# A causal convolution and two feed-forward layers on one core: earlier first transfers, zero matmuls at the start, one [high; low] stationary for the last 64 channels, the weight bound on two engines

## The chip, the cores and the metric

One core of one Trainium2 chip. The metric is the device time of one execution in microseconds. The kernel before takes 1337.52 us (median of 3 runs, 1336.18 to 1337.96); its profiled execution took 1334.66 us, of which the program's span is 1332.8 us.

## The reference

```python
w = softmax(weight, axis=-1)                     # 8 heads x 7 taps
x1 = causal_conv(x, w)                           # x: 2 x 4096 x 192, 24 channels per head
h = x1 @ w_in1                                   # 8192 x 192  @  192 x 2048
g = h * clip(h + 3, 0, 6) / 6
x2 = g @ w_out1                                  # 2048 x 192
h = x2 @ w_in2
P = a0 + a1*h + a2*h**2 + a3*h**3
Q = 1 + |b0|*|h| + |b1|*h**2
out = (P / (Q + 1e-6)) @ w_out2                  # 8192 x 192, float32
```

x is float32; the four weight matrices arrive as 64-bit floats.

## The kernel before

**Tiles.** The 8192 tokens are cut into chunks of 512 (the last one into two of 256), tokens in the free dimension and channels on the partitions. The 192 channels do not fit 128 partitions: "A" is channels 0 to 127, "B" the last 64. The 2048 hidden channels are 16 tiles f of 128. Every number is carried as a high part (rounded to the type fp32r) and a low part (the rest), and a product is high x high + low x high + high x low, so one hidden tile costs five matmuls of 128x512 in `product_in` (L481: Ah·ah, Al·ah, Ah·al and two for B) and five in `product_out` (L495 to L500).

**B before.** For layer 1 the moving tile x1b is [high; low] of the 64 channels, and the stationary tiles are Bh = [high; high] and Bl = [low; 0]. For layer 2 the moving tiles are x2m2 = [a copy of the high part; low] and x2m1, and the stationary ones Bh = [high; high] and Bl = [low; high]. `hi_w` therefore copies each piece of a weight tile twice into Bh (L369, L370) and, in layer 2, a third time into Bl (L372).

**Weights.** Each 64-bit weight is turned into a 32-bit float on the chip, per tile "in" (512 or 256 columns) or "out" (384): ACT takes the magnitude of the upper word into a box m (`mag_w`, L328), POOL bounds it between two limits (`clamp_w`, L337), DVE does three bit operations into PSUM bank 2 or 3 (`bits_w`, L349, L352, L356), ACT rounds to the high parts (`hi_w`, L363 to L372), DVE subtracts for the low parts (`lo_w`, L380). There are 16 "in" and 16 "out" tiles over both layers, and this decoding runs beside the first two chunks' layer 1.

**Start.** The filter: `weight` is loaded (tap), DVE computes the softmax into `line`, `line` is written to memory (line_d, L879) and read back as a band matrix (L268), both on ACT's queue. `conv` (L428) multiplies band with x (xn, loaded at L415, L418 on SP's queue), ACT evicts (`conv_ev`, L436), `flip` (L443) transposes, ACT and DVE make the high and low parts (L448; x1al L454, x1b L457). Chunks 0 and 1 go through this one after the other, through the same banks 0 and 1 (bank_93 and bank_94 in the lists of instructions below), before the first `product_in`.

**Steady state.** Layer 1 of one chunk and layer 2 of an earlier one are interleaved, tile by tile. A layer-1 tile costs two ACT, one DVE and one POOL instruction (L525, L530, L537, L543), a layer-2 tile about seven ACT, five DVE and two to three POOL instructions. At the end of a chunk `x2_op` (L554 to L562) takes the accumulators acc00 and acc01 to the tiles of layer 2.

**Order.** No engine's order is written out. `Issue.order` sorts all operations with tables of offsets (OFF, OFF0, OFFT, W1P, W2P, WPART, XW ...) and durations written in the code, and lets an engine take a ready operation out of turn within a look-ahead (AHEAD, LOOK). Changing any table changes the order on all engines. The DMA queues of SP and ACT are in order too: an issue that waits holds all issues behind it.

Of the kernel before, what the change touches and what calls it, by code (L numbers as in the profile page):

```python
# [46 lines left out]
X0 = -3.5576  # L47
XW = [-98.6812, -95.7871, -90.8177, -84.1979]
BIAS = dict(l1=1.5372, dec=1.797, conv=1.4061, out=-0.7086, x2=3.0264)
AHEAD = dict(P=4.733, A=25.052, V=17.217, G=15.336, S=999.0)  # L50
LOOK = dict(P=3, A=156, V=132, G=410, S=0)
OFF = dict(
    sq=-0.2391, q1=-0.0381, q2=0.2567, mm3=-0.423, mm1=0.8404, mm4=0.4459, tr=0.6018, mm2=0.8241, A=-0.3233,
    t1=0.075, u=0.9885, R=0.5331, RR=0.6369, hi2=1.4938, hi1=1.9951, S=-0.1322, lo2=1.926, lo1=2.8291,
    q=-3.2594, t2=0.1782, t3=0.4844, w=0.7884, p2=0.8597, G=0.9565, g=1.2626, cv=0.9616, x1ah=1.0094,
    x1al=1.7783, x1bh=1.0281, x1bl=1.2078, x2ah=1.7232, x2al=2.0125, x2mh=1.2801, x2mc=2.4281, x2ml=1.7914,
    oa=0.6663, oc=0.8609, os=1.4993, mm2l=1.1909, mm4l=0.5848,
# [875 lines left out]
```

## Time and profile before

| | us |
|---|---|
| device time, median of 3 | 1337.52 |
| profiled execution | 1334.66 |
| its span | 1332.8 |
| PE busy | 1268.9 (95%) |
| ACT busy | 1188.3 (89%) |
| DVE busy | 1172.6 (88%) |
| POOL busy | 1127.3 (85%) |
| first matmul of the convolution | at 15.50 |
| first `product_in` of layer 1 | at 28.68 |
| first `product_in` of layer 2 | at 126.49 |

A matmul's record is longer than the distance between two starts, so the busy time of PE in a stretch hides short gaps; where that matters, matmuls are counted and multiplied by the distance. The waits of an engine are put down to whoever came last by the records.

### The profile page before, as it was taken

What the parts mean: (1) busy time and instruction counts of PE and PEld (TensorE: products, weight loads), DVE (VectorE), ACT (ScalarE), POOL (GpSimd) and SP (SyncE); (2) the same over time, 40 slices, a digit from 0 to 9 for tenths busy, and PEclk for the clock granted to TensorE, in tenths of its full rate; (3) what the DMA queues carried; (4) which work ended last, traced back from release to release, by engine and by line L of the source; (5) the groups of instructions that cost most, each with busy time, mean ns of one, the idle gap of its engine ahead of it and who ended that gap; (6) DMA issues with size and microseconds to landing.
All of it is one profiled execution on the core that took longest, in us unless ns stands there. A gap on an engine that the chain in (4) does not pass through costs nothing.

```text
span 1332.8 us, 18555 instructions
## 1 busy us (share of the span) xinstructions
PE 1268.9 (95%) x6048; PEld 1042.9 (78%) x6048; DVE 1172.6 (88%) x1824; ACT 1188.3 (89%) x2174; POOL 1127.3 (85%) x932
## 2 busy tenths in 40 slices
PE   4988999999999999999999999999999999999977
PEld 3766887878878888788878888788788888887766
DVE  5888889899898988889999899988889888898897
ACT  4878999999999999999999999999999999998886
POOL 3977888888888889898888888888888888888875
PEclk8999999999999999999999999999999999999998
DMA  6341000000000000000000000000000000000000
GB/s 194 103 130 48 16 0 14 14 9 20 1 26 2 13 16 13 15 7 7 15 12 16 13 16 9 5 16 12 16 13 1 13 1 1 12 1 12 1 13 12
DMA packets 28984, 28.61 MB, mean 21 GB/s; under 512 B 2140, under 2 KB 25816, under 8 KB 28888
## 3 DMA queue, kind: packets, MB, share of 16 engines
q1 hardware_dynamic: 27672, 26.74, 6.6%
q8 instruction: 47, 0.77, 0.2%
q10 hardware_dynamic: 1216, 0.70, 0.2%
q14 instruction: 49, 0.40, 0.1%
HBM read 21.13 MB, written 6.30 MB: 21 GB/s over the span
## 4 chain that ended last, share of the span: by engine, by line
PE 73%; DVE 9%; ACT 9%; POOL 5%; issue 3%; DMA 0%; ACTq 0%; DVEq 0%; POOLq 0%
PE bank L481 35%; PE acc L495 7%; PE acc L498 7%; PE acc L500 7%; PE acc L499 7%; PE acc L496 7%; PE bank L428 2%; DVE S L645 1%; DVE bank L649 1%; POOL g2l L669 1%; POOL S L625 1%; DVE T L654 1%; ACT bank L640 1%; POOL g1l L543 1%; PE bank L443 1%
## 5 line engine op out<-in xcount | busy, mean ns | idle before, releaser
L625 POOL TENSOR_TENSOR S<-A,S 128x512 f32<-128x512 f32 x252 | 326.9, 1297 | 57.7 <-ACT S L611 45.2
L669 POOL TENSOR_TENSOR g2l<-T,g2h 128x512 fp32r<-128x512 f32 x252 | 328.7, 1305 | 44.2 <-ACT g2h L660 42.0
L543 POOL TENSOR_TENSOR g1l<-u,g1h 128x512 fp32r<-128x512 f32 x240 | 312.0, 1301 | 26.3 <-ACT g1h L537 21.2
L645 DVE SCALAR_TENSOR_TENSOR S<-S,bank 128x512 f32<-128x512 f32 x252 | 172.8, 686 | 85.5 <-ACT bank L640 83.0
L631 DVE SCALAR_TENSOR_TENSOR T<-T,coef,bank 128x512 f32<-128x512 f32 x252 | 188.5, 748 | 8.8
L619 DVE SCALAR_TENSOR_TENSOR T<-T,coef,bank 128x512 f32<-128x512 f32 x252 | 187.0, 742 | 8.6 <-ACT T L604 7.2
L649 DVE SCALAR_TENSOR_TENSOR bank<-T,coef,bank 128x512 f32<-128x512 f32 x252 | 188.7, 749 | 0.0
L654 DVE SCALAR_TENSOR_TENSOR T<-S,bank 128x512 f32<-128x512 f32 x252 | 173.1, 687 | 8.5
L530 DVE SCALAR_TENSOR_TENSOR u<-u,bank 128x512 f32<-128x512 f32 x240 | 162.7, 681 | 16.5 <-ACT u L525 15.3
L636 ACT ACTIVATE A<-S 128x512 f32<-128x512 f32 x252 | 159.7, 634 | 18.2 <-POOL S L625 17.2
L604 ACT ACTIVATE T<-bank,coef 128x512 f32<-128x512 f32 x252 | 173.6, 689 | 1.6 <-POOL g2l L669 1.3
L660 ACT ACTIVATE g2h<-T 128x512 fp32r<-128x512 f32 x252 | 160.2, 636 | 12.5 <-DVE T L654 10.6
L640 ACT ACTIVATE bank<-A 128x512 f32<-128x512 f32 x256 | 154.2, 603 | 14.7 <-DVE T L631 8.7
L525 ACT ACTIVATE u<-bank 128x512 f32<-128x512 f32 x240 | 143.7, 600 | 22.4 <-PE bank L481 15.1
L537 ACT ACTIVATE g1h<-u 128x512 fp32r<-128x512 f32 x240 | 150.9, 633 | 4.1 <-PE acc L500 2.3
L613 POOL TENSOR_SCALAR S<-A,coef 128x512 f32<-128x512 f32 x126 | 97.9, 777 | 43.1 <-ACT A L592 42.1
L481 PE MATMUL bank<-x2ah,Ah 128*128 128x512 f32 (+1 forms) x272 | 106.4, 391 | 16.9 <-DVE T L654 16.6
L495 PE MATMUL acc<-g2l,O 128*128 128x512 f32 (+1 forms) x280 | 112.6, 404 | 4.2 <-POOL g2l L669 2.3
L481 PE MATMUL bank<-x1ah,Ah 128*128 128x512 f32 (+1 forms) x272 | 106.2, 390 | 5.9 <-DVE u L530 2.6
L498 PE MATMUL acc<-g2h,O 128*128 128x512 f32 (+1 forms) x280 | 109.4, 391 | 0.1
L500 PE MATMUL acc<-g2h,O 128*128 128x512 f32 (+1 forms) x280 | 107.4, 384 | 0.2 <-DVE oac L677 0.2
L499 PE MATMUL acc<-g2h,O 128*128 128x512 f32 (+1 forms) x280 | 107.3, 383 | 0.0
(122 smaller groups left out, 3301.6 us busy)
## 6 DMA issues: line engine op xcount, KB each, us to landing
raw<-in_moe_w_out_dram SPq DMA_DIRECT2D x16, 384.0 KB, 3.4
out_dram<-osb SPq DMA_DIRECT2D x32, 192.0 KB, 2.0
xn<-in_x_dram SPq DMA_DIRECT2D x14, 384.0 KB, 3.4
raw<-in_moe_w_in_dram SPq DMA_DIRECT2D x16, 256.0 KB, 2.8
raw<-in_moe_w_in_dram SPq DMA_DIRECT2D x16, 128.0 KB, 3.1
xn<-in_x_dram SPq DMA_DIRECT2D x16, 96.0 KB, 3.2
xn<-in_x_dram SPq DMA_DIRECT2D x2, 288.0 KB, 5.6
band<-line_d ACTq DMA_DIRECT2D x1, 512.0 KB
```

What stands on the lines that cost most here:

```text
L481: nc.tensor.matmul(out=dst[:, cs], lhsT=w[nm][:, fs], rhs=m, start=(k == 0), stop=(k == 4))
L495: nc.tensor.matmul(out=a, lhsT=o[:, 0:128], rhs=g, start=False, stop=sp)
L498: nc.tensor.matmul(out=a, lhsT=o[:, 0:128], rhs=g, start=st, stop=False)
L499: nc.tensor.matmul(out=a, lhsT=o[:, 256:384], rhs=g, start=False, stop=False)
L500: nc.tensor.matmul(out=c, lhsT=o[:, 128:256], rhs=g, start=st, stop=False)
L543: nc.gpsimd.tensor_tensor(out=gl, in0=v1.pop((b, i)), in1=f32(g1[b, i][0]), op=ALU.subtract)
L619: stt(out=d["T"], in0=d["T"], scalar=coef[:, 2:3], in1=h2[b, i], op0=ALU.add, op1=ALU.mult)
L625: (nc.gpsimd if k else nc.vector).tensor_tensor(out=d["S"], in0=d["A"], in1=d["S"], op=ALU.add if k == 1 else ALU.mult)
L631: stt(out=d["T"], in0=d["T"], scalar=coef[:, 1:2], in1=h2[b, i], op0=ALU.add, op1=ALU.mult)
L649: stt(out=h2[b, i], in0=v2[b, i]["T"], scalar=coef[:, 0:1], in1=h2[b, i], op0=ALU.add, op1=ALU.mult)
L654: stt(out=d["T"], in0=d["S"], scalar=2.0, in1=h2.pop((b, i)), op0=ALU.subtract, op1=ALU.mult)
L669: e.tensor_tensor(out=gl, in0=v2.pop((b, i))["T"], in1=f32(gh), op=ALU.subtract)
```

## The change

The diff, cut to what acts; all tables of offsets have other numbers, of which four lines stand here.

```diff
-CONV2 = 1.7151
+CONV2 = 0.8376
-LOENG = [0, 0, 0, 0]
-CLAMP = [1, 1, 1, 1]
+WARM = 5
+LOENG = [0, 1, 0, 1]
+CLAMP = [0, 1, 0, 1]
...
-    xt = ctx.enter_context(tc.tile_pool(name="xt", bufs=2))
+    xt = ctx.enter_context(tc.tile_pool(name="xt", bufs=3))
...
+    idle = cst.tile([128, C], F32, name="idle")
+    def warm():
+        if not spare:
+            spare.append(pa.tile([128, C], F32, tag="acc11", name="warm"))
+        nc.tensor.matmul(out=spare[0], lhsT=idle[:, 0:128], rhs=idle, start=True, stop=True)
...
     def load_band():
-        nc.scalar.dma_start(
+        nc.sync.dma_start(
...
-            Bh=wts.tile([128, DFF], F32R, name=f"Bh{l}"), Bl=wts.tile([128, DFF], F32R, name=f"Bl{l}"),
+            B=wts.tile([128, DFF], F32R, name=f"B{l}"),
...
+    def bound_w(key):
+        r = raw[key]
+        e, m = (nc.gpsimd, r[2]) if CLAMP[side_of(key)] else (nc.vector, r[3])
+        e.tensor_scalar(out=m, in0=m, scalar1=LIM[0], scalar2=LIM[1], op0=ALU.max, op1=ALU.min)
+    def side_of(key):
+        return 2 * key[1] + (key[0] == "out")
...
-            act(out=w["Bh"][0:64, cs], in_=src, func=ACTF.Copy)
-            act(out=w["Bh"][64:128, cs], in_=src, func=ACTF.Copy)
-            if l == 1:
-                act(out=w["Bl"][64:128, cs], in_=src, func=ACTF.Copy)
+            act(out=w["B"][0:64, cs], in_=src, func=ACTF.Copy)
...
-            sub(w["Bl"][0:64, cs], m[hs, 256:512], w["Bh"][hs, cs])
+            sub(w["B"][64:128, cs], m[64 * part - 64:64 * part, 256:512], w["B"][0:64, cs])
...
+    low1 = [wts.tile([128, C], F32R, name=f"low1{k}") for k in range(3)]
+    low2 = [wts.tile([128, C], F32R, name=f"low2{k}") for k in range(3)]
+    def zero_low(k):
+        nc.gpsimd.memset(f32((low1 + low2)[k][64:128]), 0.0)
...
-        if l == 0:
-            seq = [("Ah", ah), ("Al", ah), ("Ah", al), ("Bh", bb), ("Bl", bb)]
-        else:
-            seq = [("Ah", ah), ("Al", ah), ("Ah", al), ("Bh", m2), ("Bl", m1)]
+        seq = [("Ah", ah), ("Al", ah), ("Ah", al), ("B", bh), ("B", bl)]
...
         elif nm == "x2mh":
-            act(out=t, in_=c, func=ACTF.Copy)
+            act(out=t[0:64], in_=c[0:64], func=ACTF.Copy)
+        elif nm == "x2mg":
+            act(out=t[64:128], in_=c[0:64], func=ACTF.Copy)
...
-            nc.vector.tensor_copy(out=t[0:64], in_=f32(x2[b, "x2m1"][0:64]))
+            nc.vector.tensor_tensor(out=t[0:64], in0=c[64:128], in1=f32(t[0:64]), op=ALU.add)
...
-        at(-100 + b if first else t - 8, "S", 1900, load_x, b, w=[("xn", b)], after=1700)
+        at(-100 + 45 * b if first else t - 8, "S", 1900, load_x, b, r=[("line_d", 0)] if b else [], w=[("xn", b)], after=1700)
...
-    at(-62, "A", 400, lambda: nc.scalar.dma_start(out=line_d, in_=line), r=[("line", 0)], w=[("line_d", 0)], after=1600)
-    at(-60, "A", 400, load_band, r=[("line_d", 0)], w=[("band", 0)], after=3600)
+    at(-62, "S", 400, lambda: nc.sync.dma_start(out=line_d, in_=line), r=[("line", 0)], w=[("line_d", 0)], after=1700)
+    at(-60, "S", 1800, load_band, r=[("line_d", 0)], w=[("band", 0)], after=1700)
...
+    for k in range(WARM):
+        at(-104 + 0.01 * k, "P", 900, warm, r=[("idle", 0)], w=[("acc11", "warm")])
```

B's stationary is now one tile [high; low] for both layers, used twice running: by the moving tile [high; high] and by [low; 0], whose zeros six memsets write once. ACT makes both halves of [high; high]: two evictions of 64 partitions in place of one for x1, and two in place of one of 128 for x2. In layer 2 the low part is the remainder of the accumulator's upper half plus its lower half. The bound moves from POOL to DVE, in PSUM, for the "in" tiles; the low parts of the "out" tiles move from DVE to POOL. Tiles of layer 2 have three buffers instead of two.

SP's queue at the start; raw is a weight tile, xn the input of a chunk (three DMAs for chunk 0). Before:

```order
L316 DMA raw<-in_moe_w_out_dram 128x2x384
L415 DMA xn<-in_x_dram 122x192
L418 DMA xn<-in_x_dram 128x3x192
L418 DMA xn<-in_x_dram 128x192
L418 DMA xn<-in_x_dram 128x4x192
L418 DMA xn<-in_x_dram 128x192
L308 DMA raw<-in_moe_w_in_dram 128x512
L313 DMA raw<-in_moe_w_in_dram 64x512 x2
L316 DMA raw<-in_moe_w_out_dram 128x2x384
L308 DMA raw<-in_moe_w_in_dram 128x512
```

After:

```order
L324 DMA raw<-in_moe_w_out_dram 128x2x384
L421 DMA xn<-in_x_dram 122x192
L424 DMA xn<-in_x_dram 128x3x192
L424 DMA xn<-in_x_dram 128x192
L316 DMA raw<-in_moe_w_in_dram 128x512
L321 DMA raw<-in_moe_w_in_dram 64x512 x2
L895 DMA line_d<-line 8x256
L277 DMA band<-line_d 128x8x128
L324 DMA raw<-in_moe_w_out_dram 128x2x384
L424 DMA xn<-in_x_dram 128x4x192
L424 DMA xn<-in_x_dram 128x192
L898 DMA coef<-in_moe_a_dram 128x4
```

The filter's line and band came from ACT's queue and go through SP's now, behind the first two weight tiles and chunk 0 alone; chunk 1 and the other weights stand behind them.

DVE from the first weight tile to chunk 0's low parts (x1al; x1b before and low after, its row for B). Before:

```order
L349 TENSOR_SCALAR bank_95<-m 128x384
L352 SCALAR_TENSOR_TENSOR bank_95<-raw,bank_95 128x384
L356 SCALAR_TENSOR_TENSOR bank_95<-raw,bank_95 128x384
L349 TENSOR_SCALAR bank_96<-m 128x512
L380 TENSOR_TENSOR O_115<-bank_95,O_115 128x2x128
L380 TENSOR_TENSOR O_115<-bank_95,O_115 128x2x64
L352 SCALAR_TENSOR_TENSOR bank_96<-raw,bank_96 128x512
L349 TENSOR_SCALAR bank_95<-m 128x384
L356 SCALAR_TENSOR_TENSOR bank_96<-raw,bank_96 128x512
L352 SCALAR_TENSOR_TENSOR bank_95<-raw,bank_95 128x384
L380 TENSOR_TENSOR Al_112<-bank_96,Ah_111 128x256
L356 SCALAR_TENSOR_TENSOR bank_95<-raw,bank_95 128x384
```

and after:

```order
L359 TENSOR_SCALAR bank_95<-m 128x384
L362 SCALAR_TENSOR_TENSOR bank_95<-raw,bank_95 128x384
L366 SCALAR_TENSOR_TENSOR m<-raw,bank_95 128x384
L341 TENSOR_SCALAR bank_96<-bank_96 128x512
L359 TENSOR_SCALAR bank_96<-bank_96 128x512
L362 SCALAR_TENSOR_TENSOR bank_96<-raw,bank_96 128x512
L366 SCALAR_TENSOR_TENSOR bank_96<-raw,bank_96 128x512
L387 TENSOR_TENSOR Al_113<-bank_96,Ah_112 128x256
L387 TENSOR_TENSOR B_114<-bank_96,B_114 64x256 x2
L470 TENSOR_TENSOR x1al<-bank_93,x1ah 128x512
L473 TENSOR_TENSOR low_120<-bank_94,x1b 64x512
```

Before, the second "out" tile (again bank_95) is decoded ahead of x1al, which comes two rows after the last one shown; after, only the first two tiles are, and an extra TENSOR_SCALAR, the bound, stands ahead of the "in" tile's bits.

POOL, from the first weight tile on; m is the box of a tile, g1l and g2l are low parts of hidden tiles of chunks 0 and 1. Before:

```order
L337 TENSOR_SCALAR m<-m 128x384
L337 TENSOR_SCALAR m<-m 128x512
L337 TENSOR_SCALAR m<-m 128x384
L337 TENSOR_SCALAR m<-m 128x256
L337 TENSOR_SCALAR m<-m 128x384
L337 TENSOR_SCALAR m<-m 128x512
L337 TENSOR_SCALAR m<-m 128x384
L543 TENSOR_TENSOR g1l<-u,g1h 128x512
L337 TENSOR_SCALAR m<-m 128x512
L543 TENSOR_TENSOR g2l<-T,g2h 128x512
L543 TENSOR_TENSOR g1l<-u,g1h 128x512
```

and after:

```order
L341 TENSOR_SCALAR m<-m 128x384
L387 TENSOR_TENSOR O_115<-m,O_115 128x2x128
L387 TENSOR_TENSOR O_115<-m,O_115 128x2x64
L341 TENSOR_SCALAR m<-m 128x384 x2
L387 TENSOR_TENSOR O_115<-m,O_115 128x2x128
L387 TENSOR_TENSOR O_115<-m,O_115 128x2x64
L387 TENSOR_TENSOR O_115<-m,O_115 128x2x128
L387 TENSOR_TENSOR O_115<-m,O_115 128x2x64
L555 TENSOR_TENSOR g1l<-u,g1h 128x512
L341 TENSOR_SCALAR m<-m 128x384
L555 TENSOR_TENSOR g2l<-T,g2h 128x512
L555 TENSOR_TENSOR g1l<-u,g1h 128x512
```

Every second bound is gone, and each "out" tile has two subtractions here, ahead of and between the hidden tiles' low parts.

## Rows read from the trace of the kernel before

**Rows 1.** The page's chain of work that ended last, shares of the span by engine.
```profile
PE 73%; DVE 9%; ACT 9%; POOL 5%; issue 3%; DMA 0%; ACTq 0%; DVEq 0%; POOLq 0%
```
**Rows 2.** Three stretches: length, busy us (instructions) by engine, granted clock, DMA share, GB/s.
```profile
28.68:126.49 97.81, 86.72 (x367) 66.27 (x367) 84.28 (x182) 76.96 (x167) 80.03 (x61) 0.98 0.35 106
200.00:300.00 100.00, 97.60 (x445) 78.30 (x446) 90.46 (x135) 91.97 (x167) 85.40 (x72) 1.00 0.04 13
1200.00:1333.00 133.00, 109.28 (x679) 95.77 (x678) 111.77 (x169) 107.57 (x193) 99.03 (x84) 0.95 0.03 9
```
**Rows 3.** The chain of waits in order of time, first 30 us: start us, us, what.
```profile
5.64 5.25 DMA line_d<-line
10.91 0.41 ACTq L268
...
15.50 3.36 PE bank L428 x16
...
20.83 0.47 DVE bank L356
...
21.62 0.61 DVE x1al L454
...
22.27 3.40 PE bank L428 x16
...
28.68 1.65 PE bank L481 x3
```
**Rows 4.** Timeline of PE, first layer-2 product and a later convolution: start, us, instruction.
```profile
126.49 0.39 PE L481 MATMUL bank<-x2ah,Ah 128*128 128x512 f32 x1
...
130.57 0.39 PE L495 MATMUL acc<-g1l,O 128*128 128x512 f32 x1
...
139.08 1.01 PE L428 MATMUL bank<-xn,band 128*122 128x120 f32 x8
139.86 0.48 PE L498 MATMUL acc<-g2h,O 128*128 128x512 f32 x1
```
**Rows 5.** Single microseconds at the start, columns as in Rows 2 (PE first, clock seventh).
```profile
16.00:17.00 1.00, 1.00 (x7) 1.00 (x6) 1.00 (x4) 0.23 (x1) 1.00 (x2) 1.00 0.41 84
...
23.00:24.00 1.00, 1.00 (x7) 1.00 (x6) 0.97 (x4) 0.47 (x2) 0.54 (x1) 0.50 0.81 238
...
30.00:31.00 1.00, 1.00 (x4) 0.71 (x4) 1.00 (x3) 0.00 (x0) 0.28 (x1) 0.50 0.94 256
```
**Rows 6.** Instruction groups of the whole run: busy us, mean ns, idle time before, releasers.
```profile
L543 POOL TENSOR_TENSOR g1l<-u,g1h 128x512 fp32r<-128x512 f32 x240 | 312.0, 1301 | 26.3 <-ACT g1h L537 21.2 <-issue 3.3 <-PE acc L496 0.5
L337 POOL TENSOR_SCALAR m<-m 128x384 f32<-128x384 f32 (+2 forms) x32 | 47.5, 1495 | 24.4 <-ACT m L328 18.6 <-ACT coef L277 5.5 <-PE bank L481 0.3
L349 DVE TENSOR_SCALAR bank<-m 128x384 int32<-128x384 int32 (+2 forms) x32 | 17.8, 555 | 10.2 <-POOL m L337 9.5
L562 DVE CAST x2m<-x2m 64x512 fp32r<-64x512 f32 (+1 forms) x17 | 12.8, 755 | 0.0
L380 DVE TENSOR_TENSOR O<-bank,O 128x256 fp32r<-128x256 f32 (+1 forms) x32 | 9.9, 350 | 0.1
L558 ACT ACTIVATE x2m<-acc 128x512 fp32r<-128x512 f32 (+1 forms) x17 | 9.7, 570 | 1.7 <-PE acc L496 1.7
L380 DVE TENSOR_TENSOR Al<-bank,Ah 128x256 fp32r<-128x256 f32 x16 | 6.7, 421 | 5.4 <-ACT Bl L372 2.2 <-ACT Bh L370 2.2 <-ACT Ah L365 1.0
L380 DVE TENSOR_TENSOR Bl<-bank,Bh 64x256 fp32r<-64x256 f32 x16 | 6.7, 421 | 3.9 <-ACT Bl L372 1.9 <-ACT Bh L370 1.7
L370 ACT ACTIVATE Bh<-bank 64x256 fp32r<-64x256 f32 x16 | 6.1, 379 | 0.2
L372 ACT ACTIVATE Bl<-bank 64x256 fp32r<-64x256 f32 x8 | 2.9, 366 | 0.0
```
**Rows 7.** The page's DMA issues: KB each, median us from issue to landing.
```profile
raw<-in_moe_w_out_dram SPq DMA_DIRECT2D x16, 384.0 KB, 3.4
out_dram<-osb SPq DMA_DIRECT2D x32, 192.0 KB, 2.0
```

More of the change, by code (lines that the diff above doesn't have):

```diff
@@ L46 @@
 D2T = 5
[L47 to L51, printed above, removed]
-OFF = dict(
[L53 to L57, printed above, removed]
+X0 = -3.2557
+XW = [-105.8871, -99.8168, -59.3715, -39.2955]
+BIAS = dict(l1=1.4587, dec=0.1797, conv=1.8628, out=-1.4432, x2=1.2507)
+AHEAD = dict(P=17.791, A=45.084, V=20.941, G=8.591, S=999.0)
+LOOK = dict(P=2, A=178, V=216, G=370, S=0)
+OFF = dict(
+    sq=-0.3729, q1=0.1602, q2=0.1324, mm3=-0.5533, mm1=0.6027, mm4=0.1407, tr=0.0986, mm2=0.6086, A=-0.3875,
+    t1=0.044, u=0.6074, R=0.2641, RR=0.5103, hi2=1.3561, hi1=1.7136, S=-0.3298, lo2=1.7039, lo1=2.0429,
+    q=-3.3751, t2=0.4308, t3=0.5046, w=0.5725, p2=0.7126, G=0.8821, g=1.0717, cv=0.9695, x1ah=0.9925,
+    x1al=1.3455, x1bh=0.4453, x1bl=1.3457, x2ah=1.2164, x2al=2.2036, x2mh=1.1366, x2mg=2.4352, x2mc=2.0761,
+    x2ml=1.54, oa=0.8735, oc=1.0231, os=1.0155, mm2l=0.8969, mm4l=0.5707,
 )
@@ L211, in conv_moe_moe_kernel @@
     bank = [ps.tile([128, C], F32, name=f"bank{k}") for k in range(4)]
-    rings = dict(u=2, g1h=2, g1l=2, S=2, T=2, A=2, g2h=2, g2l=2, x1ah=3, x1al=3, x1b=3, x1bl=3, x2ah=2, x2al=2, x2m1=2, x2m2=2, x2m2c=2,
+    rings = dict(u=2, g1h=2, g1l=2, S=2, T=2, A=2, g2h=2, g2l=2, x1ah=3, x1al=3, x1b=3, x1bl=3, x2ah=3, x2al=3, x2m1=3, x2ml=3,
                  xn=2, x1n0=1, x1n1=1, raw=4, m=5, acc00=1, acc01=1, acc10=1, acc11=1)
@@ L353, in bits_w @@
         else:
-            if not LOENG[2 * key[1] + (key[0] == "out")]:
+            if not LOENG[side]:
                 r[2], mi = p, pi
@@ L443, in flip @@
             nc.tensor.transpose(c[:, col:col + SEG], x1n[b][:, k, lo:hi], rev)
+    low1 = [wts.tile([128, C], F32R, name=f"low1{k}") for k in range(3)]
+    low2 = [wts.tile([128, C], F32R, name=f"low2{k}") for k in range(3)]
+    def zero_low(k):
+        nc.gpsimd.memset(f32((low1 + low2)[k][64:128]), 0.0)
     def x1_hi(b, part):
-        tag = ("x1ah", "x1b")[part]
-        x1[b, tag] = t = xp.tile([128, C], F32R, tag=tag, name=tag)
-        act(out=t[0:64] if part else t, in_=x1p[b, part], func=ACTF.Copy)
+        tag = "x1b" if part else "x1ah"
+        if (b, tag) not in x1:
+            x1[b, tag] = xp.tile([128, C], F32R, tag=tag, name=tag)
+        t = x1[b, tag]
+        act(out=t[64 * part - 64:64 * part] if part else t, in_=x1p[b, min(part, 1)], func=ACTF.Copy)
     def x1_lo(b, part):
-        c = x1p.pop((b, part))
+        c = x1p[b, part]
         if part == 0:
@@ L518, in mm1 @@
             bl, c0, n = units[b]
-            product_in(0, b, i, [x1[bl, k][:, c0:c0 + n] for k in ("x1ah", "x1al", "x1b")], h1[b, i])
+            product_in(0, b, i, [x1[bl, k][:, c0:c0 + n] for k in ("x1ah", "x1al", "x1b", "x1bl")], h1[b, i])
         @staticmethod
@@ L579, in mm3 @@
             h2[b, i] = bank[site2(b, i)[2]]
-            product_in(1, b, i, [x2[b, k] for k in ("x2ah", "x2al", "x2m1", "x2m2")], h2[b, i])
+            product_in(1, b, i, [x2[b, k] for k in ("x2ah", "x2al", "x2m1", "x2ml")], h2[b, i])
         @staticmethod
@@ L860, in conv_moe_moe_kernel @@
             at(tt + where[("x1ah", "x1bh")[hf]], "A", 478, x1_hi, b, hf, r=[key], w=[xh], kind="conv")
+            if hf:
+                at(tt + where["x1bh"] + 0.002, "A", 478, x1_hi, b, 2, r=[key], w=[("x1bg", b)], kind="conv")
             at(tt + where[("x1al", "x1bl")[hf]], "V", 602, x1_lo, b, hf, r=[key, xh], w=[xl_], kind="conv")
```

118 lines of the change are left out of this document (55 added, 63 removed).

## The prediction

> **What bounds the kernel now.** I read first the shares of the chain of waits: PE holds 73% of the chain, DVE and ACT 9% each [rows 1]. So a saving counts where PE waits, and an addition on ACT or DVE counts mostly where those engines end last. Next, the busy time by stretches. In a steady hundred microseconds PE is busy 97.6, DVE 90.5, ACT 92.0, POOL 85.4 [rows 2]; there is little to win there unless the matmuls themselves become shorter, and the same 20 matmuls per hidden tile stay. PE is free at both ends. At the start the first `product_in` comes at 28.68 us [rows 3]. From there to the first layer-2 product at 126.49 [rows 4] lie 97.8 us. PE's recorded busy time says 86.7 there [rows 2], but a record is 0.39 long and the next starts earlier: from 126.49 to 130.57 there are 18 starts' distances, 0.227 us each [rows 4]. In the order 340 matmuls of 128x512 stand ahead of 126.49, 77.1 us, and one chunk's convolution (1.6, at 0.78 for 8 records [rows 4]) and transposes: PE has some 18 us of waits there. DVE is the busiest besides PE (84.3 of 97.8) while it decodes weights [rows 2]. In the last 133 us PE is busy 109.3, DVE 111.8, ACT 107.6 [rows 2]: the remaining layer-2 tiles wait on each other's chain.
>
> **The start.** The chain to the first convolution is: `line` ready at 5.64, its store to memory landed at 10.9 (5.25 us), band issued at 10.91, convolution at 15.50 [rows 3]. The change removes nothing of this; it puts less ahead of it. By the sizes in the code some 1.75 MB had been issued by 5.64 before, and 1.55 MB after (chunk 1's 0.48 MB is gone, the rest of the first "in" tile comes in). The store: at most the 5.25 us it took, at least the 2.0 us of a store to the output later in the run [rows 7]; I take 3.6, the middle, since most of what stood ahead still does. Band: at most 4.6 us (10.91 to 15.50, with two weight tiles beside it), at least the 3.4 us of a 384 KB weight tile [rows 7]; I take 4.2, nearer the upper end because the pieces are small and unchanged. The convolution then starts at 5.65 + 3.6 + 4.2 = 13.5: **gain 2.0** (0 to 4.4).
>
> Here a rule of the Trainium skill speaks against the change. The row: line_d was on ACT's queue behind perm alone and still took 5.25 us [rows 3]. "DMA: Bandwidth & Descriptors", section "Queues, rings and completion order", says that each DMA engine takes packets in turn from the queue rows that have work, SP and ACT each owning a row that is consumed in ring order; by it, moving the line to SP's row puts it behind all that SP issued. The row does not show the advantage that the line should have had on ACT's row; by the rule the gain of 2.0 would be 0, which is the end of the range already.
>
> What waits behind: SP now holds the second "out" tile, chunk 1 and the coefficients until band is issued, at about 9.3. Chunk 1's convolution is wanted at 22.27 before [rows 3], about 19.6 after; even at 5.25 us the transfer is there by 15.5. If the line landed 4 us later, that cover would be gone.
>
> From the first convolution to the first `product_in` it took 13.2 us [rows 3]. DVE made chunk 0's x1al at 21.62, behind the second "out" tile's bits at 20.83 [rows 3]; after, that decode stands behind x1al. I count **0.8** (0 to 1.5): half a bit operation and the two ACT copies that go ahead of x1ah. The first two tiles' decode no longer waits for ACT to issue band, and ends before x1al is due: cost nothing.
>
> The zeros: five matmuls of four passes, ten records; a 128x512 record at half clock is 0.43 apart (four in 30 to 31 us at 0.50 [rows 5]), twice that for two passes each, so at most 9 us from about 1.5, ending before 11: on an idle PE, cost 0. What they give: the convolution of chunk 0 ran 16 records in 3.36 although the clock is recorded as 1.00, the same rate as chunk 1's at 0.50 (seven in a microsecond both times [rows 5]), while a later one takes 0.78 for 8 (139.08 to 139.86 [rows 4]). So both convolutions ran at the 1.2 GHz level, and 1.8 us each is to be had. But the clock was at 0.50 again in 30 to 31 us [rows 5], after the second convolution and a pause, and the zeros end some 3 us ahead of band. I take 0, to 3.6.
>
> **The decode stretch.** ACT loses the second and third copies, 6.1 + 2.9 = 9.0 us [rows 6]. DVE waited for these copies 2.2 + 2.2 ahead of Al and 1.9 + 1.7 ahead of Bl, 8.0 us in all [rows 6]; one B copy per piece remains, so I take 5 (0 to 8). DVE's own work: 16 bounds at the 555 ns of the bit operation that resembles it, +8.9; subtractions of the "out" tiles, -9.9; -1.0 net. POOL: 16 bounds of 1495 ns go, -23.9; 32 subtractions come, for which no POOL row has this size: 0.98 us per "out" tile if the 1301 ns of 128x512 scales with 384 columns, 2.6 if an instruction costs 1301 whatever its size [rows 6]. I take 1.2, near the scaled end, because the bounds' 1495 ns for 384 columns on average, the same engine's other form, is not far from scaling: +19.2, net -4.7. So DVE, which ends the stretch, has 6 us less to do and to wait for, of 18 us that PE waits. Not all is on the path, since the tables reorder everything: **gain 4** (2 lost to 9).
>
> **Steady state and end.** ACT gets one eviction of 64 partitions more per chunk for x1 and one for x2, 33 at about 570 ns as the one for x2m [rows 6], 18.8 us. ACT holds 9% of the chain [rows 1]: **loss 1.7** (0 to 7: with ACT free about 8 us in 100, a third exposed is the worst that I see). DVE's copy into x2m, 755 ns [rows 6], becomes an addition from PSUM of the size of the subtraction ahead of it: under 2 us in the run, mostly hidden, **gain 0.2**. The third buffer for layer 2's tiles removes a wait that no row shows: 0. The end's new tables: 0, 4 either way; the order has 33 layer-2 products behind the last layer-1 product before and after.
>
> Sum: -2.0 - 0.8 - 4 + 1.7 - 0.2 = -5.3 us on the profiled execution's 1334.66 (span 1332.8 and 1.9 around it), 1329.4. The median of the runs is 2.9 above that execution, so 1337.5 - 5.3 = **1332** for the median.
>
> **The rivals.** (a) The clock stays up: band comes early enough after the zeros, and both convolutions run at the 2.4 GHz level: 3.6 more, 1328. For it: PE has less pause than before. Against: the pauses between the steps remain.
> (b) The decode stretch gives nothing: the "in" tile's chain on DVE is one operation longer, and DVE, 84.3 of 97.8 busy, gets only 1.0 less to do. Then -2.8 + 1.7 - 0.2 = -1.3: 1336, no change that a measurement of this kernel can tell (0.2%, 2.7 us).
> (c) Slower: POOL becomes the bound of the decode stretch. It is busy 80.0 of 97.8 [rows 2]. At 2.6 us per "out" tile it has 80.0 - 23.9 + 41.6 = 97.7, all of the stretch, and its queue is in order, so the hidden tiles' low parts (1.3 us each, for which PE waits) stand behind subtractions. It decides from 1.5 us per tile, where the bound that went is used up. With half of the 17.7 us on the path instead of the gain of 4: -2.8 + 8.9 + 1.5, 1345.
> (d) Slower: ACT's 18.8 us are exposed by half in the steady state, because x2's second eviction stands up to 14 ACT instructions behind the first and holds the accumulator: +9.4 instead of +1.7, 1340.
> (e) The second use of B needs no load of its own and saves time: two neighbouring starts are 0.227 apart, 512 columns at 2.4 GHz take 0.213; 544 pairs by 0.014 are 7 us, 1325. "TensorE: Matmul & The Clock Gate", section "Part 2: What happens when you issue a matmul", says that one load can serve repeated matmuls. Against: before, the program has as many loads as matmuls, and each hides beside a matmul.
>
> **How the numbers follow.** Forecast 0.50, (a) 0.10, (b) 0.20, (c) 0.09, (d) 0.07, (e) 0.04. Faster by over 0.2%: the forecast, (a) and (e), 0.64. Same: (b), 0.20. Slower: (c) and (d), 0.16. The range reaches from 1322 ((a) with the better end of the decode stretch) to 1341 ((d) in, (c) left out).
>
> **What would show it.** Right: the convolution starts between 12 and 15, the first `product_in` between 24 and 27.5; the first layer-2 product 5 to 9 us earlier; PE as busy in the middle as before. Wrong: a start at 15.5 (the line waits on SP's queue as it did on ACT's), a POOL row for the "out" subtractions above 1.5 us a tile with PE waiting for it, more PE waits per hundred microseconds in the middle, or conv records 0.1 apart from the beginning (rival a).

## The result: slower by 0.7%, and where the time went

The changed kernel takes 1346.82 us (median of 4 runs, 1343.39 to 1347.59) beside 1336.85 for the kernel before: a ratio of 1.007, 95% interval 1.005 to 1.009. The forecast was 1332. The profiled execution took 1347.13 us, its span is 1345.3; that of the kernel before was 1332.8, so 12.5 us are to be found.

The page's chain of the changed kernel, shares by engine; PE holds more of it than before [rows 1], and DVE less:

```profile
PE 77%; ACT 10%; DVE 6%; POOL 3%; issue 2%; DMA 1%; POOLq 0%; DVEq 0%; ACTq 0%
```

Three stretches of it (length, then busy us of PE, PEld, DVE, ACT, POOL, granted clock, DMA share, GB/s), as in [rows 2]; the first again runs from the first `product_in` to the first layer-2 product:

```profile
28.37:122.74 94.37, 87.23 (x362) 64.91 (x363) 84.01 (x170) 72.01 (x149) 75.86 (x74) 0.98 0.37 111
200.00:300.00 100.00, 96.98 (x435) 78.16 (x434) 88.18 (x132) 92.13 (x168) 84.11 (x71) 0.98 0.03 10
1200.00:1345.00 145.00, 123.41 (x774) 108.89 (x773) 122.57 (x185) 119.87 (x217) 110.91 (x94) 0.95 0.03 9
```

The start and decode stretch is shorter than before, as wanted. But in the middle PE fell from 97.60 to 96.98 in a hundred microseconds, and from 445 to 435 matmuls; a fall of the granted clock at 210 us, which lies in this window, is most of that difference (1.7 us of full-rate time, some 7 matmuls).

**A measure that the order can't disturb.** The two kernels put their work in different orders, so equal events don't mean equal progress (335 matmuls stand ahead of the first layer-2 product now, 340 before). I therefore took every matmul of 512 or 256 columns in a trace and subtracted from its start the PE work that stands ahead of it in program order: 0.2265 us per 128x512 (the distance of two starts), 0.115 per 256 columns, and the convolutions and transposes at their full-rate distances. What is left is the time that PE has *lost* up to there: waits, slow clock and start together. PE's work is 1219.4 us in both, so the kernel before loses 113.4 us in all and the changed one 125.9:

| us lost by PE | before | changed |
|---|---|---|
| up to the first layer-2 product | 41.7 | 39.1 |
| up to the 100th us of PE's work | 41.9 | 42.2 |
| from the 100th to the 1100th ("the middle") | 28.2 | 41.3 |
| after the 1100th | 43.3 | 42.4 |

The whole loss lies in the middle, 13.1 us. PE's waits there, from 200 to 1200 us (us in total, times, longest), of the kernel before:

```profile
PE bank L481 <- DVE T L654: 4.0, 5, 0.9
PE bank L481 <- ACT osb L693: 1.7, 3, 0.8
PE acc L495 <- POOL g2l L669: 1.3, 4, 0.5
PE acc L498 <- ACT g1h L537: 1.3, 2, 1.1
```

and of the changed kernel:

```profile
PE bank L493 <- DVE T L669: 12.2, 13, 1.8
PE acc L510 <- ACT g2h L675: 2.3, 5, 0.6
PE acc L507 <- POOL g2l L684: 2.1, 3, 0.9
PE acc L510 <- DVE x2al L569: 1.0, 2, 0.5
```

Thirteen waits for T, the last product on DVE of a layer-2 tile, in some thirteen chunks; they rose by 8.2 us. They stand at the end of a chunk's layer 1, where `x2_op` empties the accumulators. Its pieces on ACT are x2ah (L567) for channels A, and x2mh (L571) and the added x2mg (L573) for the two halves of [high; high]; on DVE they are x2al (L569), and x2ml (L575) and x2mc (L577) for B's low part. One of the waits, with DVE, ACT and PE of the changed kernel around 455 us (start, us, instruction, and in brackets the idle time ahead and who ended it):

```profile
453.39 0.75 DVE L646 SCALAR_TENSOR_TENSOR T<-T,coef,bank 128x512 f32<-128x512 f32 x1
454.17 0.68 DVE L575 TENSOR_TENSOR low<-acc,x2m 64x512 fp32r<-64x512 f32 x1
454.89 0.69 DVE L577 TENSOR_TENSOR low<-acc,low 64x512 fp32r<-64x512 f32 x1
455.61 0.69 DVE L660 SCALAR_TENSOR_TENSOR S<-S,bank 128x512 f32<-128x512 f32 x1
456.22 0.75 DVE L664 SCALAR_TENSOR_TENSOR bank<-T,coef,bank 128x512 f32<-128x512 f32 x1
457.00 0.69 DVE L669 SCALAR_TENSOR_TENSOR T<-S,bank 128x512 f32<-128x512 f32 x1
```

```profile
453.56 0.58 ACT L571 ACTIVATE x2m<-acc 64x512 fp32r<-64x512 f32 x1
454.04 0.58 ACT L567 ACTIVATE x2ah<-acc 128x512 fp32r<-128x512 f32 x1
454.52 0.58 ACT L655 ACTIVATE bank<-A 128x512 f32<-128x512 f32 x1
...
457.21 0.59 ACT L573 ACTIVATE x2m<-acc 64x512 fp32r<-64x512 f32 x1
```

```profile
455.58 0.39 PE L508 MATMUL acc<-g2l,O 128*128 128x512 f32 x1
457.74 0.50 PE L493 MATMUL bank<-x2ah,Ah 128*128 128x512 f32 x1 [1.78 <-DVE T L669]
```

ACT puts two evictions of the accumulators ahead of L655 and DVE the two operations for x2's low part ahead of L660, L664 and L669, the end of a layer-2 tile's chain; only L669 gives the bank back to PE. Here DVE is what is late: it runs from L646 to L669 without a gap, and x2ml and x2mc are 1.4 us of that, while the added eviction comes only at 457.21. In another chunk the added eviction itself is ahead:

```profile
370.44 0.59 ACT L573 ACTIVATE x2m<-acc 64x512 fp32r<-64x512 f32 x1
```

```profile
371.06 0.68 DVE L575 TENSOR_TENSOR low<-acc,x2m 64x512 fp32r<-64x512 f32 x1 [0.90 <-ACT x2m L573]
```

```profile
374.62 0.79 PE L493 MATMUL bank<-x2ah,Ah 128*128 128x512 f32 x1 [1.77 <-DVE T L669]
```

DVE stands idle for 0.90 us until x2mg has ended, then runs without a gap to the L669 that PE waits for. DVE waited for x2mg in this way in four chunks of the middle, 3.3 us in all. In two chunks PE's pause was followed by a fall of the granted clock (columns: length, PE busy, clock, DMA share, GB/s), 1.7 us of full-rate time each; the pause of 1.78 above was not. The kernel before has no fall in the middle, so the falls are 3.4 of the 13.1 us:

```profile
211.00:212.00 1.00, 1.00 (x4) 0.50 0.00 0
...
376.00:377.00 1.00, 1.00 (x4) 0.50 0.00 0
```

### The profile page after: what moved, and what is told of

It is laid out like the page before. It is cut to its first block, busy times and chain, and to the rows that moved or that the text cites. A ratio compares the mean times of both kernels' runs of the same rounds, so it can differ in the third digit from the quotient of the medians.

```text
span 1345.3 us, 18628 instructions
## 1 busy us (share of the span) xinstructions
PE 1284.9 (96%) x6058; PEld 1049.4 (78%) x6058; DVE 1173.5 (87%) x1808; ACT 1195.6 (89%) x2183; POOL 1121.0 (83%) x954
## 4 chain that ended last, share of the span: by engine, by line
PE 77%; ACT 10%; DVE 6%; POOL 3%; issue 2%; DMA 1%; POOLq 0%; DVEq 0%; ACTq 0%
PE bank L493 37%; PE acc L510 7%; PE acc L512 7%; PE acc L507 7%; PE acc L511 7%; PE acc L508 7%; PE bank L434 2%; ACT A L607 2%; POOL S L640 1%; PE bank L449 1%; ACT T L619 1%; ACT A L651 1%; POOL g2l L684 1%; ACT g2h L675 1%; ACT bank L655 1%
## 5 line engine op out<-in xcount | busy, mean ns | idle before, releaser
L684 POOL TENSOR_TENSOR g2l<-T,g2h 128x512 fp32r<-128x512 f32 x252 | 326.5, 1296 | 38.7 <-ACT g2h L675 36.3
L660 DVE SCALAR_TENSOR_TENSOR S<-S,bank 128x512 f32<-128x512 f32 x252 | 173.1, 687 | 95.0 <-ACT bank L655 92.1
L493 PE MATMUL bank<-low,B 128*128 128x512 f32 (+1 forms) x544 | 206.6, 380 | 0.2 <-DVE low L577 0.2
L646 DVE SCALAR_TENSOR_TENSOR T<-T,coef,bank 128x512 f32<-128x512 f32 x252 | 188.4, 747 | 8.2
L664 DVE SCALAR_TENSOR_TENSOR bank<-T,coef,bank 128x512 f32<-128x512 f32 x252 | 188.8, 749 | 0.0
L669 DVE SCALAR_TENSOR_TENSOR T<-S,bank 128x512 f32<-128x512 f32 x252 | 173.0, 687 | 8.5
L655 ACT ACTIVATE bank<-A 128x512 f32<-128x512 f32 x256 | 154.1, 602 | 14.2 <-DVE T L646 9.9
L493 PEld LDWEIGHTS bank<-low,B 128*128 128x128 f32 x544 | 103.4, 190 | 19.8 <-DVE low L577 0.5
L510 PE MATMUL acc<-g2h,O 128*128 128x512 f32 (+1 forms) x280 | 110.9, 396 | 3.8 <-ACT g2h L675 3.5
L507 PE MATMUL acc<-g2l,O 128*128 128x512 f32 (+1 forms) x280 | 109.9, 394 | 4.5 <-POOL g2l L684 4.4
```

The costliest lines, as they stand in the source:

```text
L493: nc.tensor.matmul(out=dst[:, cs], lhsT=w[nm][:, fs], rhs=m, start=(k == 0), stop=(k == 4))
L507: nc.tensor.matmul(out=a, lhsT=o[:, 0:128], rhs=g, start=False, stop=sp)
L510: nc.tensor.matmul(out=a, lhsT=o[:, 0:128], rhs=g, start=st, stop=False)
L646: stt(out=d["T"], in0=d["T"], scalar=coef[:, 1:2], in1=h2[b, i], op0=ALU.add, op1=ALU.mult)
L660: stt(out=d["S"], in0=d["S"], scalar=c1, in1=h2[b, i], op0=ALU.add, op1=ALU.mult)
L664: stt(out=h2[b, i], in0=v2[b, i]["T"], scalar=coef[:, 0:1], in1=h2[b, i], op0=ALU.add, op1=ALU.mult)
```

## The experiments

Two causes were at hand: the **tables** (another order) and the **evictions** (33 more on ACT). All runs are collected here; "middle" is the loss from the 100th to the 1100th us of PE's work in the profiled execution, "up to 100" the loss before it, and the ratio is to the kernel before on the same chip. A middle is that of one execution: in e6, g3, g5 and g6 it is the kernel's fastest, 10.5 us under the median in e6 and some 3 in the others.

| kernel | median us | ratio, 95% | up to 100 | middle |
|---|---|---|---|---|
| before | 1336.85 | 1 | 41.9 | 28.2 |
| before, second trace (g4) | one run | | 48.4 | 27.9 |
| changed | 1346.82 | 1.005 to 1.009 | 42.2 | 41.3 |
| changed, again (f1) | 1346.99 | 1.0058 to 1.0088 | 42.4 | 40.9 |
| before + changed tables (e3) | 1339.27 | 1.0011 to 1.0035 | 43.8 | 34.4 |
| before + two evictions (e8) | 1338.05 | 1.0006 to 1.0025 | 44.6 | 31.4 |
| before, x2_op sooner (e4) | 1340.84 | 1.0009 to 1.0039 | 47.7 | 33.5 |
| changed, x2_op later (e1) | 1350.84 | 1.0092 to 1.0125 | 41.6 | 47.7 |
| e1, x2mg beside x2mh (g3) | 1353.61 | 1.0109 to 1.0143 | 39.1 | 42.5 |
| changed, copies by DMA (e5) | 1338.49 | 1.0009 to 1.0029 | 40.1 | 34.8 |
| only x2's by DMA (e6) | 1345.61 | 1.0057 to 1.0091 | 37.2 | 37.8 |
| only x1's by DMA (e7) | 1338.41 | 1.0003 to 1.0030 | 42.4 | 36.3 |
| changed + tables of before (f2) | 1339.68 | 1.0008 to 1.0028 | 43.0 | 35.4 |
| f2, x2_op sooner (g2) | 1346.99 | 1.0054 to 1.0098 | 39.5 | 42.8 |
| changed without zeros (f3) | 1346.90 | 1.0057 to 1.0087 | 42.7 | 41.5 |
| both repairs (f4) | 1334.85 | 0.9965 to 0.9986 | 41.2 | 30.4 |
| f4 again (g6) | 1334.17 | 0.9968 to 0.9997 | 37.6 | 30.4 |
| f4 without zeros (g1) | 1335.46 | 0.9974 to 0.9997 | 43.9 | 30.9 |
| g1, memsets behind line (g5) | 1334.26 | 0.9973 to 0.9992 | 38.2 | 30.8 |

**The tables and x2_op's place.** First, one number of the changed kernel went back, x2_op's priority (e1), and the same number was brought into the kernel before (e4); then the changed steady tables as a whole into the kernel before (e3). The start and the last unit keep their own tables in all of these.

```diff
 # e1: the changed kernel; e4: the kernel before, with 1.2507
-        self.ops.append((..., t + BIAS.get(kind, 0.0)))
+        self.ops.append((..., t + (3.0264 if kind == "x2" and HEAD <= t < LASTT else BIAS.get(kind, 0.0))))
```

> The changed kernel, with one number other: from planner time 19.5 to the last unit the operations of x2_op (the accumulators to layer 2's tiles) get the bias 3.0264 of the kernel before in place of 1.2507, so that they give way to layer 2's chain. The changed kernel lost 15.4 us over 13 chunks (985.8 to 1001.2 from the first to the fourteenth output); 11.6 of these are PE waits, most of them one wait a chunk of 0.5 to 1.9 us for DVE's T (L669), where x2ml and x2mc stand back to back on DVE ahead of w, p2 and G. Theory 1 (the place of x2_op in the order makes the loss): that wait is gone, 76 us a chunk, 1333 to 1339 in all. Theory 2 (ACT's 33 evictions more make it, whatever the order): 1344 to 1348. Theory 3 (the other tables make it): 1344 to 1348 too, told from 2 by the next run. A bias so high can also hold the accumulators too long: then a wait of acc (L510) for x2_op shows in place of the one for T.

> The kernel before with the steady tables of the changed one, its own structure (Bh, Bl, one eviction for x2m) and its own start and end. Theory 1 and theory 3 (order): the loss comes along, 1345 to 1352, with PE waits for DVE's T at each chunk's x2_op. Theory 2 (structure): 1335 to 1340.

> The kernel before, with one number other: the bias of x2_op 1.2507 (the changed kernel's) in place of 3.0264, in the steady part alone. Theory 1 (place of x2_op): most of the loss comes along, 1343 to 1350. Theory 3 (other tables) and theory 2 (structure): 1335 to 1340.

Theory 1 (x2_op's place makes the loss) fell in its first form: e1 is slower still, 1350.84. In e3 the tables alone cost the kernel before 6.2 us in the middle (28.2 to 34.4, one clock fall of 1.7 among it), and 2.8 us of the median; in e4 x2_op's priority alone costs 5.3 (again with one fall). So a part of the loss is order, but not all of it, and a priority that is right for one set of tables is wrong for another.

**The evictions.** The second half of [high; high] was copied from SBUF to SBUF by a transfer in place of ACT's second eviction, for both layers (e5), for x2 alone (e6), for x1 alone (e7), x1's from chunk 2 on; and the kernel before got ACT's load without anything else (e8: two evictions of 64 partitions per chunk made twice).

```diff
 # e5 (x2; x1 alike), the changed kernel
-            act(out=t[64:128], in_=c[0:64], func=ACTF.Copy)
+            nc.sync.dma_start(out=f32(t[64:128]), in_=f32(t[0:64]))
```

> The changed kernel, but from chunk 2 on the second half of [high; high] is not a second eviction by ACT: SP requests a copy of the first half from SBUF to SBUF, for x1 and for x2, so that ACT has as many evictions per chunk as in the kernel before. All tables stay. The runs so far: the changed tables on the kernel before cost 0.2% (13 chunks 986.4 us against 985.7), so the order alone is not the cause. Theory 2 (ACT's two evictions more per chunk, 2 x 0.57 us, are exposed nearly in full, 14.8 us in 13 chunks): 13 chunks in 984 to 990 us, 1330 to 1337 in all, and one PE wait a chunk for DVE's T less. Theory 4 (the rest of the structure: x2mc as an addition from PSUM, which keeps the accumulator, and the tiles of zeros): 13 chunks stay at 998 to 1003, 1343 to 1348.

> The changed kernel, only x2's second half copied by a transfer from SBUF to SBUF; x1's second eviction stays on ACT. Theory 2: half of the gain of the run with both, 1337 to 1342. If the place at the end of a chunk is what counts (x2's eviction stands in layer 2's chain there, x1's does not): all of the gain, 1331 to 1338. Theory 4: 1343 to 1348.

> The changed kernel, only x1's second half copied by a transfer; x2's second eviction stays on ACT. Theory 2: the other half of the gain, 1337 to 1342. If the place at the end of a chunk counts: nothing, 1343 to 1348.

> The kernel before with ACT's load of the changed one and nothing else of it: from chunk 2 on x1's eviction of channels B is made twice, and 64 partitions of x2m's are written once more (the same values). Theory 2: 13 chunks take 10 to 16 us longer than 985.7, 1345 to 1353 in all. Theory 4: 1336 to 1340.

e5 takes 8.3 us off the changed kernel, and the middle loses 34.8 instead of 41.3. Its waits for T from 200 to 1200 us, as above:

```profile
PE bank L496 <- DVE T L672: 9.5, 12, 1.6
```

By the middle's losses x1's eviction was worth 5.0 (e7) and x2's 3.5 (e6), so the place at the end of a chunk is not what alone makes an eviction dear. In the medians x1's copy brings the whole gain (8.4) and x2's 1.2, which is within the noise. e6's six executions lie between 1335.14 (mean granted clock 0.994, the profiled one) and 1345.70 (0.983), four of them above 1345.5; the 3.5 comes from the fastest, so what x2's eviction costs is not shown. e8 contradicts theory 2 as it stood: the same load costs the kernel before only 1.9 us of the median and 3.2 in the middle, not 10 to 16. A second eviction takes time of ACT and also reads its bank or accumulator longer; a transfer ends both, and no run separates them.

**Do they add?** The changed kernel with the steady tables of the kernel before (f2; a first form of it, e2, gave no time), with both repairs (f4), and unaltered again (f1):

```diff
 # f2: from planner time 19.5 to the last unit; f4: this and e5's transfers
-AHEAD, LOOK, OFF, BIAS of the changed kernel
+AHEAD, LOOK, OFF, BIAS of the kernel before; x2mg=1.2811
```

> The changed kernel unaltered, beside the next three on the same chip, for a second trace of it. By a count of PE's work against the clock time (0.2265 us per 128x512), between 100 and 1100 us of PE's work it lost 41.3 us where the kernel before lost 28.2; the kernel before with the changed tables lost 34.4, with two evictions more on ACT 31.4, and the changed kernel with its copies by transfers 34.8. Theory A (tables about +6 and evictions about +6, that add): this stretch loses 38 to 45 us again, 1343 to 1348 in all. Theory B (chance: falls of the clock that differ from execution to execution): another trace shows other falls, and the stretch loses under 36 us in it.

> The changed kernel with the steady tables (OFF, AHEAD, LOOK, BIAS) of the kernel before from planner time 19.5 to the last unit, x2mg right behind x2mh; start and last unit keep the changed tables. Theory A (tables and evictions add): the tables' 6 us come back, 1338 to 1342, 32 to 36 us lost in the middle stretch. Theory C (the evictions are dear only under the changed tables, as the two evictions more cost the kernel before 1.9 us): 1333 to 1338. Theory D (the structure apart from the evictions costs): 1343 to 1348.

> The changed kernel's start and structure with both repairs: copies of the second halves by transfers from SBUF to SBUF, and the steady tables of the kernel before. Theory A: both losses gone, 1329 to 1335, the middle stretch 26 to 31 us lost. If the start gains nothing on average, 1335 to 1338. Theory D: over 1340.

Nearly. The middle repeats within 0.6 us over three traces of the changed order (41.3, 40.9, 41.5 with f3), so it is not chance. From f4's 30.4, the changed tables add 4.4 (e5), the evictions 5.0 (f2), and both 10.9. In the medians, each taken against the kernel before on its own chip, 5.3, 4.8 and 12.1. So 1.5 to 2 us come only with both. The waits for T of f2 and, with the copies by transfer, of f4:

```profile
PE bank L506 <- DVE T L682: 13.6, 15, 1.2
```

```profile
PE bank L509 <- DVE T L685: 7.9, 13, 1.1
```

So the evictions reach PE largely through the waits for T. f4's are still thirteen, but shorter, none followed by a fall of the clock in the middle. f4 and its repeat are 0.25% and 0.18% faster than the kernel before: the best version here.

**Which entry of the tables?** f2 with x2_op's priority at the changed value (g2), and e1 with x2mg placed right behind x2mh (g3).

```diff
 # g2, in f2's tables
-BIASN = dict(l1=1.5372, dec=1.797, conv=1.4061, out=-0.7086, x2=3.0264)
+BIASN = dict(l1=1.5372, dec=1.797, conv=1.4061, out=-0.7086, x2=1.2507)
```

> The changed kernel with the steady tables of the kernel before, as run already (1339.7, 35.4 us lost in the middle stretch), but x2_op's bias at the changed 1.2507. Theory A1 (the tables' price is x2_op's earlier place, x2ml and x2mc back to back in layer 2's chain): the price is back, 40 to 43 us lost, 1344 to 1348. Theory A2 (it is spread over the other offsets): 34 to 37 us, 1338 to 1341.

> The changed kernel with x2_op's bias at 3.0264 as in the first run (1350.8, 47.7 us lost in the middle stretch), but x2mg right behind x2mh instead of far behind it. If the late second eviction was that run's trouble (theory A1 stands): 34 to 38 us lost, 1338 to 1342. If the other tables do not bear x2_op so late: 44 to 49 us, 1348 to 1352.

> The kernel before unaltered, for a second trace of the stretch by which all others are measured. By the changed kernel's three traces (41.3, 40.9 and 41.5 us lost) the middle stretch is the same from execution to execution: 27 to 30 us lost again (28.1 in the first trace). The start can differ: the four traces with this start had 41.7 to 47.5 us lost at the first layer-2 product.

g2 brings the whole price back, 42.8 us in the middle and 1346.99: with the other offsets of the kernel before, x2_op's earlier place is the tables' loss. Its waits for T, 17.3 us in 15:

```profile
PE bank L506 <- DVE T L682: 17.3, 15, 2.6
```

g3 shows the other side: the changed tables lose 42.5 also with x2_op late, and the median is 1353.61. Against e1 (47.7, 1350.84) the earlier x2mg took 5.2 off the one traced middle and nothing off the median. Which other offset needs it early was not found.

**The start.** The zeros were left out (f3), and POOL was to be held back until the filter was ready (g1, where its memsets still ran beside the filter, and g5, where they did not).

```diff
 # g5, in f4, zeros removed; g1 copied line[:, 0:1], which only line's memset writes
-    for k in range(6): at(-98 + k, "G", 600, zero_low, k, w=[("low", k)])
+    at(-72, "G", 100, lambda: nc.gpsimd.tensor_copy(out=gate, in_=line[:, SEG - 1:SEG]), ...)
+    for k in range(6): at(-70 + k, "G", 600, zero_low, k, r=[("gate", 0)], w=[("low", k)])
```

> The changed kernel without the five matmuls of zeros; all other instructions keep their order. In the changed kernel's trace the clock is at half from 12 to 30 us, in its sister with x2's copy by a transfer only from 14 to 18, and 4.6 us less are lost up to the 80th us of PE's work. If the zeros move the clock's fall into the convolution and the transposes: the first product_in within 0.5 us of the changed kernel's, but half clock in other stretches, and the time 2 to 5 us lower, 1341 to 1345. If they do nothing: as the changed kernel within 1 us. If they keep PE at full rate where it would be slow: 1 to 4 us higher.

> The last kernel (copies by transfers, steady tables of the kernel before) with the start altered: no zeros, no memset of their operand, and POOL's six memsets behind a one-column copy of line, so that POOL stands still while DVE computes the filter. In the changed kernel DVE's TENSOR_SCALAR of 8x7 took 0.45 us beside POOL's memsets and 0.16 after them, and line was stored at 6.7 in place of 5.64. If POOL's work is the cause: these operations 0.16 to 0.22, line at 5.6, convolution at 13.2 to 13.6 (14.66 in the last kernel), the time up to 1 us less, 1333 to 1335. If the operations are slow for another reason: line at 6.7, convolution at 14.4 to 14.7. The first bound of a weight tile stands on POOL behind the memsets; if the decoding waits for it, the gain at the convolution is given back by the first product_in.

> As the run with the memsets behind a copy of line, but the copied column is now one that DVE's last filter operation writes (before, it was one that only line's memset writes, and POOL's memsets still ran from 1.6 to 4.5). If POOL's work makes DVE's TENSOR_SCALAR slow: all of them 0.16 to 0.28, line stored at 5.5 to 5.9, convolution at 13.2 to 13.7. If not: 6.7 and 14.4 to 14.7. The memsets and the bound of the first weight tile then stand 4 us later on POOL, so the time is within 1.5 us of 1334.9 either way.

> The version with both repairs once more (copies by transfers, steady tables of the kernel before), beside the run above: 1333 to 1337, 0.1 to 0.35% below the kernel before, and 29 to 32 us lost in the middle stretch.

Without zeros the time is the same: 1346.90 beside 1346.99 of f1 on the same chip, first `product_in` at 28.57 instead of 28.37. g5 shows what delayed `line`. POOL and DVE of the changed kernel:

```profile
1.31 2.91 POOL L456 MEMSET low<- 64x512 f32 x6
...
2.32 0.45 DVE L258 TENSOR_SCALAR tmp<-tap,one 8x7 f32<-8x7 f32 x1
2.80 0.46 DVE L259 TENSOR_SCALAR tmp<-tmp 8x7 f32<-8x7 f32 x1
3.29 0.45 DVE L261 TENSOR_SCALAR tmp<-tmp 8x7 f32<-8x7 f32 x1
3.78 0.15 DVE L262 SCALAR_TENSOR_TENSOR tmp<-tmp,tmp 8x7 f32<-8x7 f32 x1
...
4.35 1.34 DVE L267 SCALAR_TENSOR_TENSOR tmp<-tmp,tmp 8x7 f32<-8x7 f32 x6
4.99 1.49 POOL L341 TENSOR_SCALAR m<-m 128x384 f32<-128x384 f32 x1 [0.78 <-ACT m L336]
```

and the same operations in g5, with POOL's memsets from 6.87 on:

```profile
3.57 0.16 DVE L273 TENSOR_SCALAR tmp<-tmp 8x7 f32<-8x7 f32 x1
3.76 0.16 DVE L275 TENSOR_SCALAR tmp<-tmp 8x7 f32<-8x7 f32 x1
```

The filter takes 3.47 us from its first operation to the last (3.13 to 6.60) instead of 4.55 (2.13 to 6.68). `weight` happened to arrive 1 us later in g5's trace, so the convolution came no earlier (14.99), and the time equals that of g6: that an earlier filter saves time is not shown.

## Why the prediction was wrong, step by step

- **The start's transfers: right in size, in part by luck.** The store of `line` took 3.61 (3.6 said), the band 3.96 to landing (4.2 said). The chain of the changed kernel's head, which answers to [rows 3]:

```profile
6.71 3.61 DMA line_d<-line
10.34 3.96 DMA band<-line_d
...
14.39 3.64 PE bank L434 x16
...
20.62 0.70 DVE x1al L470
...
21.36 3.67 PE bank L434 x16
...
25.68 2.31 PE bank L449 x10
```

  The line did not wait on SP's queue as it had on ACT's. But `line` was ready 1.07 late, which I had not priced, so the convolution came at 14.39 and not at 13.5: 0.82 of it are the three TENSOR_SCALAR beside POOL's memsets (six in place of one long one that was over at 2.5), 0.25 one of the six operations of L267 beside the first bound. And a later store is a shorter one: in e4, the old start with `weight` 1 us late, the store began at 6.59 and took less than the 5.25 of [rows 3] on ACT's queue too:

```profile
6.59 4.45 DMA line_d<-line
```

  So, by this one trace, about half of the 1.6 us that the store gained went with its later start.
- **From the convolution to the first `product_in`: no gain instead of 0.8 in this trace.** It took 13.98 (14.39 to 28.37), against 13.2 in [rows 3] and 14.06 in the second trace of the kernel before (16.40 to 30.46). The one execution that I read ran its convolutions in 3.36 and 3.40; four later traces of the same start show 3.64 or more. It was the best of five, which made the start look harder to beat: up to the 100th us of PE's work the old start lost 45.3 on average over its five traces, the new one 40.8 over twelve. The start and the decoding together gave some 4.5 (old 41.9 to 48.4, new 37.2 to 43.0), not 6.8. Against the one trace that the forecast started from they gave nothing: 41.9 before, 42.2 after.
- **The zeros: right** (they end at 7.94, cost nothing, and f3 shows no gain from them). Rival (a) is off in the changed kernel's trace, but its half came true elsewhere: in e6, g2 and g6 the second convolution ran in 2.23 in place of 3.67, and from the first convolution to the first `product_in` it took 11.4 to 11.5. It did so in g5 as well, which has no zeros, so the zeros are not needed for it; what decides it is not shown. In e6:

```profile
20.52 2.23 PE bank L434 x16
```

- **The decode stretch: 2.3 of 4, then given back.** The stretch from the first `product_in` to the first layer-2 product is 3.4 shorter (97.81 to 94.37), 1.1 of it because five matmuls fewer stand ahead. POOL took 1.16 us per "out" tile (1.2 said), so rival (c) is off:

```profile
L387 POOL TENSOR_TENSOR O<-m,O 128x256 fp32r<-128x256 f32 (+1 forms) x32 | 18.5, 599 | 10.8 <-ACT O L373 10.6
...
L464 ACT ACTIVATE x1b<-bank 64x512 fp32r<-64x512 f32 x32 | 18.8, 589 | 1.3 <-PE bank L449 1.1
...
L573 ACT ACTIVATE x2m<-acc 64x512 fp32r<-64x512 f32 (+1 forms) x17 | 9.6, 565 | 0.4
L571 ACT ACTIVATE x2m<-acc 64x512 fp32r<-64x512 f32 (+1 forms) x17 | 9.5, 558 | 0.6 <-PE acc L508 0.5
```

  Just behind that product PE waits for ACT's high part of layer 1, and by the 100th us of its work the lead is gone:

```profile
129.82 0.50 PE L510 MATMUL acc<-g1h,O 128*128 128x512 f32 x1 [1.77 <-ACT g1h L549]
```

- **The steady state: the step that failed.** The work was priced rightly: by the rows above and [rows 6] ACT has 9.4 us more for x1 and 9.4 more for x2, 18.8 as said. Wrong was to multiply it by ACT's 9% of the chain. The evictions cost 6.5 in the middle under the changed tables, 5.0 under the old ones. Some 26 of the 33 lie there, 14.8 us of work, so 34 to 44% of it was exposed, where I took 9% as the forecast; in the kernel before it is 22% (3.2 us, e8). The 6.5 still lies within the 0 to 7 that I gave this term, so it does not explain the miss alone. The share of the chain says where the last instruction's history ran, not what one more instruction does to a tile's chain in which ACT, DVE and PE wait for each other by turns.
- **And no term for the steady tables.** I priced the end's tables (0, 4 either way; measured 0.9 less lost) and none in the middle, where the same diff replaces OFF, BIAS, AHEAD and LOOK: 4.4 to 6.2 us. With the evictions and what only both bring, this is 10.9 of the 13.1 us of the middle.
- **Rival (d)** had the right engine, and its late x2mg is seen: DVE waits for it four times (3.3 us), and one of PE's longest waits for T follows. It is not the main cause: PE's waits from 200 to 1200 us have no entry for x2mg, x1's copy brought more than x2's, and f2, with x2mg right behind x2mh, still lost 5.0 by the evictions.
- **Rival (e)** is off: 6058 loads for 6058 matmuls (6048 for 6048 before), and the second use of B starts 0.227 behind the first, as every other matmul does.
- **The signs.** Of the signs of being right only the convolution's start came (14.39, in 12 to 15). The first `product_in` at 28.37, the first layer-2 product 3.8 earlier and PE's waits in the middle all were on the other side. The range's lower end, by its own parts (1332 less 3.6 and less 5), is 1323 and not 1322.

Open: f4 still loses 2.2 us more in the middle than the kernel before. The addition from PSUM for x2's low part may be the rest, but it was not run alone; nor was the third buffer. By the parts (13.1 in the middle, less 4.5 for an average start, less 0.9 at the end) the difference of the medians should be 7.7; it is 10.0, and the falls of the clock, which differ between executions, are not settled to that accuracy.

## What to carry to other kernels

Price an added instruction where several engines pass a tile around by the slack of that loop, not by its engine's share of the critical chain; with engines some 90% busy, 22 to 44% of it came through here. A table of order tuned for one set of instructions is part of the kernel: when a diff replaces it, give it a term of its own, and test it with the old structure and the new one. Idle DMA queues can take duplicates that an engine makes (128 KB in 2.2 us here).
